# Another order of wave 0's half-block products and of the sums around them, in a linear-attention and MLP kernel

## The chip, the cores and the metric

The kernel runs on one core of one Trainium2 chip. A core has TensorE (PE; its weight loads are shown apart as PEld), VectorE (DVE), ScalarE (ACT), GpSimd (POOL) and SyncE (SP). Each takes its instructions strictly in the order in which the program lists them, and waits on semaphores for the others. The metric is the device time of one execution in microseconds (us). Three runs of the kernel before took 193.93 to 194.47 us, with a median of 194.27.

## The reference

Attention with a decay over blocks, then an MLP. What is computed, cut to the core:

```python
# q, k, v: 4 batches, 8 heads, 768 tokens, 64 columns; blocks of 64 tokens; lam: one decay per head
intra = einsum('bhic,bhjc->bhij', qb, kb) * Dmask      # Dmask[i, j] = lam ** (i - j) for i >= j
intra = einsum('bhij,bhjd->bhid', intra, vb)
inter = einsum('bhid,bhde->bhie', qb * lam_pow, kv_state)
out[:, :, sl] = intra + inter
kv_state = lam_block * kv_state + einsum('bhsd,bhse->bhde', kb_dec, vb)

x = out.transpose(0, 2, 1, 3).reshape(B * S, H * D)    # 3072 tokens, 512 columns
h = x @ w_in                                           # 512 x 2048
g = h * (1.0 / (1.0 + exp(-1.702 * h)))
result = g @ w_out                                     # 2048 x 512
```

## The kernel before, in words

The 3072 tokens are worked off in six waves of 512. For each wave the attention makes xT (x transposed), the first MLP product with the activation makes g (g_sb: 16 chunks of 128 hidden columns by 512 tokens, bf16), and the second product with w_out makes the output. Waves 0 and 1 hold two batches each with 256 tokens of each; the halves are called c = 0 and c = 1. While the second product of one wave runs, the attention of the next is worked in between its pieces. The order is written out by hand: `steps` reads strings of short names and calls one function for each, and the whole is under a manual schedule, so the order of the program is the order of each engine's queue.

**The second product.** g is seen as a 2 by 2 matrix of blocks (token half i, hidden half kh: a11, a12, a21, a22; hidden chunks with even number are the first half) and w_out as 2 by 2 blocks (hidden half, column half: b11 to b22). Instead of eight block products there are seven, by a scheme of Strassen's kind. It needs four sums of g (`g_sums`, L439, tile g_s: s1 = a21 + a22, s2 = s1 - a11, s3 = a11 - a21, s4 = a12 - s2) and four of w_out (`weight_sums`, L426, tile w_out_t: t1 = b12 - b11, t2 = b22 - t1, t3 = b22 - b12, t4 = b21 - t2), all on DVE. The products are

- 1: a11 b11, 2: a12 b21, 3: s4 b22, 4: a22 t4, 5: s1 t1, 6: s2 t2, 7: s3 t3.

`product` (L459) issues product n for token tiles t (0, 1) and hidden pairs m (0 to 7): one matmul of 128x128 by 128x256 for each, so 16 for a whole product. They add up in three PSUM banks: X takes 1, then 6, 5 and 3 on top; V takes 7, and then 4 from zero; Q takes 2. When the last matmul of a product is issued, `after_product` empties the bank: products 1, 6 and 7 are copied by ACT to an f32 tile (L472, tile part); product 2 is added to 1, 5 to 7, and 4 to 6 by DVE (L483, tile o_sb); 3 is copied by ACT (L481). The add of product 2 is put off until the step `o`; that of 4 waits until 6 is there. Each output block is stored by two DMAs issued on SP (L489). A product that goes on in the same bank waits until the bank has been read.

**Steps and names.** `P60` is product 6 for token tile 0, `P61` for tile 1. `p6...` takes both tiles and a part of the pairs: `a` is pairs 0 to 3, `b` 4 and 5, `l` 0 to 5, `h` 6 and 7. `gl3` makes s3 for pairs 0 to 3, `gh12` makes s1 and s2 for pairs 4 to 7. `W2` makes the sums of chunk 2 of w_out. w_out comes in four chunks of 512 KB by DMAs on POOL's queue (L185); chunk j serves pairs 2j and 2j + 1, so pairs 6 and 7 need the last chunk, number 3.

**Wave 1's attention** in between. `do_cast` (L202) multiplies q or k by its decay and casts it to bf16 (ks, qs), on DVE for c = 0 and on POOL for c = 1. `turn_pe` transposes the result by eight PE matmuls (L238) and a copy of ACT (kT, qT). `cast_v` casts v (on POOL for c = 0, on ACT for c = 1). `start` runs the first state products (`d_one`, L279) with ACT's copies of them, the scores (L259) with their masks on DVE (L267, tile sm), and the first part of the output (`d_even`, L298). `end` runs the rest of the output (`d_out`, L316), more state products, and the copies to xT. `load(2, "kq")` issues four loads of wave 2 on SP. `mlp1_half` (L414) is a part of the first MLP product of wave 1, and needs a PSUM bank of the three that X, V and Q use.

The steps 5 to 13 are worked between the pieces of wave 0's first MLP product, `mlp1(0, fc)`; the loop over `halves` is wave 1's first MLP product, which follows.

Of the kernel before, what the change touches and what calls it, by code (L numbers as in the profile page):

```python
# [25 lines left out]
def kernel(  # L26
# [391 lines left out]
    half_sum, blocks, part, c11, c12 = {}, {}, {}, {}, {}  # L418
    TS = [const.tile([P, FFC // 2, d_model // 2], bf16, name=f"w_out_t{n}") for n in range(1, 5)]

    def weight_sums(j):
        b = w_out_sb[j].rearrange("p (m two) (c d) -> p two c m d", two=2, c=2)
        t1, t2, t3, t4 = (t[:, j * CW // 2 : (j + 1) * CW // 2] for t in TS)
        for o, x, y in ((t1, b[:, 0, 1], b[:, 0, 0]), (t2, b[:, 1, 1], t1),
                        (t3, b[:, 1, 1], b[:, 0, 1]), (t4, b[:, 1, 0], t2)):
            nc.vector.tensor_tensor(o, x, y, op=SUB)  # L426

    def token_half(w, i, kh):
# [134 lines left out]
    def one_step(w, s):  # L563
        if s[0] == "+":
            w, s = w + 1, s[1:]
        x, a = w + 1, s[1:]
        if s[0] == "f":
            mlp1(w, int(a))
        elif s[0] in "abcd":
            k = "abcd".index(s[0])  # L570
            in_product(w, GR[w][k], int(s[1]), TAGS[w][k], dve_copy if s[2:] == "v" else act_copy)
        elif s[0] in "ABCD":
            in_gelu(w, GR[w]["ABCD".index(s[0])], int(a))
        elif s[0] == "P":
            product(w, int(s[1]), (int(s[2]),))
        elif s[0] == "p":
            product(w, int(s[1]), (0, 1), {"a": range(4), "b": range(4, 6), "l": range(6), "h": range(6, 8)}[s[2]])
        elif s[0] == "W":
            weight_sums(int(a))
        elif s[0] == "I":  # L580
            in_sums(int(a))
        elif s[0] in "kq":
            do_cast(x, int(a), s[0], nc.vector)
        elif s[0] in "KQ":
            do_cast(x, int(a), s[0].lower(), nc.gpsimd)
        elif s[0] == "t":
            turn_dma(x, int(s[2]), s[1])
        elif s[0] == "v":
            cast_v(x, int(s[1]), ((act_copy, dve_copy)[s[2:] == "v"],))
        elif s[0] == "S":  # L590
            n_scores(x, int(a))
        elif s[0] == "M":
            n_masks(x, int(a))
        elif s[0] == "m":
            n_masks(x, int(a), True)
        elif s[0] == "R":
            n_rest(x)
        elif s[0] == "o":
            c11.pop(w)()
        elif s[0] == "X":  # L600
            x_sums(x)
        elif s[0] == "G":
            gate_pool(x_sum[w][3][0:1, 0, 0:1])
        elif s[0] == "g":
            m0, m1 = {"l": (0, 4), "h": (4, 8)}[s[1]]
            g_sums(w, m0, m1, tuple(int(c) - 1 for c in s[2:]))
        elif s[0] == "L":
            load(w + (1 if a == "w" else 2), "kq" if a == "k" else "v")
        else:
            raise ValueError(s)  # L610
# [26 lines left out]
    with tc.manual_schedule():  # L637
        for x, i in ((k_pow, i_k), (q_pow, i_q)):
            nc.scalar.activation(x, ln_lam.unsqueeze(1).to_broadcast([P, 2, H]), EXP, scale=i)
        mk_pow(inv_pow, -1.0 * P)  # L640
        for j, rows in enumerate((A, Z)):
            nc.scalar.activation(blk_pow[rows].rearrange("p (r i) -> p r i", i=2),
                                 ln_lam[rows].rearrange("p (r j i) -> p r j i", i=2, j=2)[:, :, j, :], EXP, scale=1.0 * P)
        nc.scalar.activation(warm, q_pow[:, 0, 0:1], GELU)
        fill(3)
        for nm, copies in (("k", (dve_copy, act_copy)), ("q", (act_copy, dve_copy))):
            for g in range(2):
                do_cast(0, 0, nm, nc.vector, g)
            for g in range(2):
                turn_pe(0, 0, nm, copies[g], g)  # L650
                fill(2 - g if nm == "k" else 1 - g)
        gate_pool(loaded[0, 0, "q"][0:1, H // 2, 0:1])
        load_w_in(0)
        load_one(0, 1, "v", v)
        cast_v(0, 0, (act_copy, act_copy))
        d_scores(0, 0, 0)
        d_scores(0, 0, 1)
        fill(3)
        do_cast(0, 1, "k", nc.gpsimd, 0)
        load_w_in(1)  # L660
        do_cast(0, 1, "k", nc.gpsimd, 1)
        for j in range(2, len(IN_CH)):
            load_w_in(j)
        for j in range(NCH):
            load_w_out(j)
        d_one(0, 0, "mm")
        d_keep(0, 0)
        turn_pe(0, 1, "k", act_copy, 0)
        oa, oz = d_out(0, 0, ("mm", "mm"))
        nc.scalar.copy(seen, oz[:, 3, P - 1 : P])  # L670
        d_state(0, 0, states[0, 0], Z)
        do_cast(0, 1, "q", nc.vector, 0)
        do_cast(0, 1, "q", nc.vector, 1)
        d_x(0, 0, 0, oa, act_copy)
        turn_pe(0, 1, "q", act_copy, 0)
        d_inter(0, 0, oz, 0, False)
        turn_pe(0, 1, "k", dve_copy, 1)
        turn_pe(0, 1, "q", dve_copy, 1)
        d_x(0, 0, 1, oz, act_copy)
        fill(1, "a")  # L680
        d_scores(0, 1, 0, True)
        cast_v(0, 1, (act_copy, dve_copy))
        nc.gpsimd.affine_select(mask, mask, pattern=[[0, 1], [1, P]], channel_multiplier=-1, base=0,
                                compare_op=mybir.AluOpType.is_ge, fill=0.0)
        gate_sync(w_out_sb[1][0:1, 0, 0:2])
        load(1)
        d_scores(0, 1, 1, True)
        mlp1_half(0, 0, 0)
        d_one(0, 1)
        d_keep(0, 1)  # L690
        act_copy(kv_sb[0][:, 0], states[0, 0])

        def start(w, c):
            if c == 0:
                d_one(w, c)
                d_keep(w, c)
            for pp in range(2):
                d_scores(w, c, pp)
            d_even(w, c, ("mm", "a")[c])

        def end(w, c):
            oa, oz = d_out(w, c)
            t = acc("ps_kv", shape=[P, NP, D]) if w else states[w, c]
            if w == 0:
                nc.scalar.copy(seen, oz[:, 3, P - 1 : P])
            d_state(w, c, t, Z)
            if w == 0:
                d_inter(w, c, oz, 0, False)
            if w and c == 0:
                d_one(w, 1)  # L710
            d_x(w, c, 0, oa, act_copy)
            d_x(w, c, 1, oz, act_copy if w and c else dve_copy)
            if w:
                nc.vector.tensor_tensor(kv_sb[0][:, 2 * w + c], kept[w, c], t, op=ADD)
            else:
                nc.scalar.copy(kv_sb[0][:, 2 * w + c], t)
            if w and c == 0:
                d_keep(w, 1)

        def steps(w, names):  # L720
            for s in names.split():
                one_step(w, s)

        end(0, 1)
        for c, fc in ((0, 2), (1, 0), (1, 2)):
            mlp1_half(0, c, fc)
        for fc in range(4, FFC):
            mlp1(0, fc)
            steps(0, {5: "I1", 7: "I3", 9: "I0 gl3 gl1", 11: "W0 gl2", 13: "W1 gl4"}.get(fc, ""))
        steps(0, "p1a gh3 p2a W2 p1b p2b p7l W3 p1h p2h p7h")  # L730
        do_cast(1, 0, "k", nc.vector)
        steps(0, "p4l")
        do_cast(1, 0, "q", nc.vector)
        turn_pe(1, 0, "k", act_copy)
        steps(0, "p4h gh1 gh2 o")
        load(2, "kq")
        cast_v(1, 0)
        do_cast(1, 1, "k", nc.gpsimd)
        turn_pe(1, 0, "q", act_copy)
        steps(0, "P60")  # L740
        start(1, 0)
        steps(0, "P61 gh4")
        cast_v(1, 1, (act_copy, act_copy))
        do_cast(1, 1, "q", nc.gpsimd)
        turn_pe(1, 1, "k", act_copy)
        steps(0, "P50 P51")
        end(1, 0)
        turn_pe(1, 1, "q", act_copy)
        steps(0, "P30 P31")
        halves = [(c, fc) for c in range(HF) for fc in HALVES]  # L750
        for i, (c, fc) in enumerate(halves):
            if i == 1:
                start(1, 1)
            if i == 3:
                end(1, 1)
            if i == 4:
                x_sums(1)
            mlp1_half(1, c, fc)
            if i in (1, 2, 3, 4):
                nm = "kq"[(i - 1) % 2]  # L760
                do_cast(2, (i - 1) // 2, nm, nc.gpsimd)
                turn_dma(2, (i - 1) // 2, nm)
            if i == 6:
                load(2, "v")
        steps(1, STEPS[1])
        for w in range(ND, NW):
            steps(w, STEPS[w])
# [30 lines left out]
```

## Time and profile before

| | |
|---|---|
| time, median of 3 runs | 194.27 us |
| time of the profiled execution | 195.65 us |
| span of the profiled execution | 193.9 us |
| TensorE clock granted | 1.0 of full speed |
| PE busy | 185.0 us (95% of the span) |
| PEld busy | 151.6 us (78%) |
| DVE busy | 154.1 us (79%) |
| ACT busy | 129.9 us (67%) |
| POOL busy | 54.1 us (28%) |
| HBM read and written | 27.26 MB and 6.29 MB |

The span runs from the first to the last instruction; the time of an execution also holds what lies around it. In the profile's timelines a row has the start and the duration in us, the engine, the line of the kernel, the operation, the tile written and the tiles read, the sizes and the number of instructions taken together. Square brackets give the idle time just before, and what ended it. The end of a matmul is modelled, so the durations of neighbouring PE rows overlap.

The part of the program that the change touches lies between 26 and 53 us of the span.

### The profile page before, as it was taken

To read this page: it belongs to the slowest core of one execution; us is meant where nothing else is said; L and a number is where in the kernel's file an instruction comes from. 1 tells how busy PE (TensorE), PEld (TensorE's weight loads), DVE (VectorE), ACT (ScalarE), POOL (GpSimd) and SP (SyncE) were. 2 spreads that over 40 slices of the span, in tenths; PEclk is the share of its full clock that TensorE was granted. 3 is DMA by queue.
4 is the path that set the end of the run, shared out by engine and by line. 5 is a ranking of instruction groups with operands and counts; after the bars stand their busy time and mean duration, and the time that the engine had idled before them with its cause. 6 is when DMAs were issued, how large, how long until landed. Compare 5 with 4: busy or idle time off the path is not lost.

```text
span 193.9 us, 5541 instructions
## 1 busy us (share of the span) xinstructions
PE 185.0 (95%) x2295; PEld 151.6 (78%) x2297; DVE 154.1 (79%) x292; ACT 129.9 (67%) x242; POOL 54.1 (28%) x76
## 2 busy tenths in 40 slices
PE   7889999699999999999999999999999999999993
PEld 2556646577888887888888888888888888888882
DVE  1897599589377899988899979799979797889850
ACT  4867664246677885559796389896388885587711
POOL 4498000068476000088000096000294000000000
PEclk9999999999999999999999999999999999999999
DMA  5999999998997899657798935999455903300113
GB/s 148 306 275 196 201 194 213 290 299 215 224 248 168 193 249 236 163 137 137 178 237 189 270 110 134 208 246 231 163 150 125 211 7 109 111 3 0 47 43 130
DMA packets 89599, 33.91 MB, mean 175 GB/s; under 512 B 67430, under 2 KB 89446, under 8 KB 89574
## 3 DMA queue, kind: packets, MB, share of 16 engines
q1 hardware_dynamic: 84676, 28.84, 59.4%
q0 software_dynamic: 4896, 4.72, 14.4%
q8 instruction: 18, 0.29, 0.6%
q14 instruction: 7, 0.06, 0.1%
q10 hardware_dynamic: 2, 0.00, 0.0%
HBM read 27.26 MB, written 6.29 MB: 173 GB/s over the span
## 4 chain that ended last, share of the span: by engine, by line
PE 69%; DMA 12%; DVE 9%; POOL 5%; ACT 1%; issue 1%; SPq 1%; ACTq 0%
PE ps_X L459 19%; PE ps_hX L542 16%; DMA w_out<-in_moe_w_out_dram 10%; PE ps_hV L542 8%; PE ps_V L459 7%; PE ps_hQ L542 4%; PE ps_Q L459 4%; PE ps_h L414 4%; DVE g_s L439 3%; DMA qf<-in_q_dram 3%; POOL w_in L181 2%; PE ps_s L335 2%; PE ps_o L390 2%; POOL ks L202 1%; DVE sm L348 1%; POOL w_out L185 1%
## 5 line engine op out<-in xcount | busy, mean ns | idle before, releaser
L459 PEld LDWEIGHTS <-g_s 128*128 128x128 bf16 x384 | 36.8, 98 | 6.7 <-issue 1.2
L561 ACT ACTIVATE g_sb<-h_sb 128x512 bf16<-128x512 f32 x54 | 32.6, 631 | 1.2 <-DVE h_sb L550 1.2
L459 PEld LDWEIGHTS <-g_sb 128*128 128x128 bf16 x288 | 27.5, 98 | 5.9 <-issue 1.8
L542 PEld LDWEIGHTS <-w_in_t 128*128 128x128 bf16 x288 | 28.1, 98 | 3.3
L221 ACT COPY part<-ps_hX 128x512 f32<-128x512 f32 x32 | 18.3, 586 | 11.5 <-PE ps_hX L542 11.5
L459 PE MATMUL ps_X<-w_out_t,g_s 128*128 128x256 bf16 x192 | 23.5, 273 | 0.5 <-ACT part L472 0.2
L542 PEld LDWEIGHTS <-w_in 128*128 128x128 bf16 x216 | 21.1, 98 | 2.4
L542 PE MATMUL ps_hX<-x_s,w_in_t 128*128 128x256 bf16 x144 | 21.6, 272 | 0.0
L439 DVE TENSOR_TENSOR g_s<-g_sb 128x1024 bf16<-128x1024 bf16 x24 | 16.3, 688 | 5.8 <-ACT g_sb L561 5.6
L632 POOL CAST behind_q<-x_s 1x1 f32<-1x1 bf16 x3 | 0.5, 174 | 61.7 <-DVE x_s L527 61.7
L209 POOL TENSOR_TENSOR qs<-qf,q_pow 128x512 bf16<-128x512 f32 x16 | 16.6, 1063 | 2.7 <-DMA qf<-in_q_dram 2.7
L209 POOL TENSOR_TENSOR ks<-kf,k_pow 128x512 bf16<-128x512 f32 x16 | 16.6, 1063 | 1.9 <-DMA kf<-in_k_dram 1.9
L472 ACT COPY part<-ps_X 128x512 f32<-128x512 f32 (+1 forms) x14 | 7.3, 522 | 13.9 <-PE ps_X L459 13.9
L218 DVE COPY part<-ps_hV 128x512 f32<-128x512 f32 x18 | 12.4, 688 | 4.3 <-PE ps_hV L542 4.3
L550 DVE TENSOR_TENSOR h_sb<-part,ps_hX 128x512 f32<-128x512 f32 x18 | 12.3, 681 | 2.7 <-PE ps_hX L542 2.7
L459 PE MATMUL ps_X<-w_out,g_sb 128*128 128x256 bf16 x96 | 12.6, 273 | 0.8 <-DMA w_out<-in_moe_w_out_dram 0.8
L550 DVE TENSOR_TENSOR h_sb<-part,ps_hV 128x512 f32<-128x512 f32 x18 | 12.3, 684 | 1.0 <-PE ps_hV L542 1.0
L459 PE MATMUL ps_Q<-w_out,g_sb 128*128 128x256 bf16 x96 | 12.5, 273 | 0.0
L459 PE MATMUL ps_V<-w_out_t,g_sb 128*128 128x256 bf16 x96 | 11.8, 273 | 0.7 <-ACT part L472 0.7
L550 DVE TENSOR_TENSOR h_sb<-part,ps_hQ 128x512 f32<-128x512 f32 x18 | 12.2, 679 | 0.0
L267 DVE TENSOR_TENSOR sm<-ps_s,mask_d 128x512 bf16<-128x512 f32 x14 | 8.8, 684 | 3.8 <-PE ps_s L259 3.6
L459 PE MATMUL ps_V<-w_out_t,g_s 128*128 128x256 bf16 x96 | 11.6, 273 | 0.2 <-DVE w_out_t L426 0.2
(111 smaller groups left out, 360.5 us busy)
## 6 DMA issues: line engine op xcount, KB each, us to landing
kf<-in_k_dram SPq DMA_DIRECT2D x10, 512.0 KB, 6.6
qf<-in_q_dram SPq DMA_DIRECT2D x10, 512.0 KB, 6.6
vf<-in_v_dram SPq DMA_DIRECT2D x10, 512.0 KB, 6.0
out_dram<-o_sb SPq DMA_DIRECT2D x24, 128.0 KB, 2.4
out_dram<-o_sb SPq DMA_DIRECT2D x12, 256.0 KB, 2.7
w_out<-in_moe_w_out_dram POOLq DMA_DIRECT2D x4, 512.0 KB, 14.6
kf<-in_k_dram SPq DMA_DIRECT2D x4, 256.0 KB, 3.1
qf<-in_q_dram SPq DMA_DIRECT2D x4, 256.0 KB, 5.0
```

The costliest lines, as they stand in the source:

```text
L181: nc.gpsimd.dma_start(out=w_in_sb[j], in_=moe_w_in.rearrange("(kc ki) f -> ki kc f", ki=P)[:, :, c0 : c0 + IN_CH[j] * P])
L209: eng.tensor_tensor(x.rearrange("p b (r i j d) -> p j (b r) i d", i=2, j=2, d=D)[:, j], f.rearrange("p h (a d) -> p (h a) d", a=2).rearran ...
L218: nc.vector.tensor_copy(out, in_)
L221: nc.scalar.copy(out, in_)
L267: nc.vector.tensor_tensor(sm.rearrange("p i a s -> p i (a s)"), flat, mask_d.rearrange("p o a b s -> p o (a b s)").to_broadcast([P, 2, 2 * ...
L414: nc.tensor.matmul(h[:, u, :], w_in_sb[j][:, kc, i * P : (i + 1) * P], xT[w][:, kc, cols], start=(kc == 0), stop=(kc == KC - 1))
L439: nc.vector.tensor_tensor(o, x, y, op=f)
L459: nc.tensor.matmul(bank[:, t], x[:, m, t * P : (t + 1) * P], y, start=(n in (1, 2, 7) and t == ts[0] * last and m == 0), stop=(m == FFC // ...
L472: nc.scalar.copy(part[w, n, t.start][:, t], bank[:, t])
L542: nc.tensor.matmul(bank[:, u], z[:, kc], y[:, kc], start=(n in (1, 2, 7) and u + kc == 0), stop=(kc == 1), skip_group_check=True)
L550: nc.vector.tensor_tensor(h, h_part[w, g, {2: 1, 5: 7, 4: 6}[n]], bank, op=ADD)
L561: nc.scalar.activation(g_of[w][:, a : b + 1 : b - a, 256 * i : 256 * i + 256], bank, GELU)
```

## The change

- Wave 0's second product runs its products in the order 1, 2, 7, 6, 4, 5, 3 and no longer 1, 2, 7, 4, 6, 5, 3. Product 6 is now in two pieces by pairs, product 4 in three, and its last piece comes after the second turn.
- Products 5 and 3 are split differently around wave 1's work: tile 0 of product 5 comes ahead of `start(1, 0)`, tile 1 after it; tile 0 of product 3 stands ahead of the second turn of q, and tile 1 after the first piece of wave 1's first MLP product.
- `weight_sums` takes an order. Chunks 0 and 1 keep theirs; chunk 2 runs t3, t1, t2, t4; chunk 3 runs t3, t1, t2, and t4 only after wave 1's casts of k and q.
- s1 and s2 for pairs 4 to 7 are made ahead of chunk 3's sums; s4 for these pairs is made after chunk 3's t4.
- The cast of v's half c = 1 and POOL's cast of q now stand directly after `start(1, 0)`.

```diff
-    def weight_sums(j):
+    def weight_sums(j, which=(0, 1, 2, 3)):
         b = w_out_sb[j].rearrange("p (m two) (c d) -> p two c m d", two=2, c=2)
         t1, t2, t3, t4 = (t[:, j * CW // 2 : (j + 1) * CW // 2] for t in TS)
-        for o, x, y in ((t1, b[:, 0, 1], b[:, 0, 0]), (t2, b[:, 1, 1], t1),
-                        (t3, b[:, 1, 1], b[:, 0, 1]), (t4, b[:, 1, 0], t2)):
+        ops = ((t1, b[:, 0, 1], b[:, 0, 0]), (t2, b[:, 1, 1], t1),
+               (t3, b[:, 1, 1], b[:, 0, 1]), (t4, b[:, 1, 0], t2))
+        for i in which:
+            o, x, y = ops[i]
             nc.vector.tensor_tensor(o, x, y, op=SUB)
...
-            weight_sums(int(a))
+            weight_sums(int(a[0]), tuple(int(i) - 1 for i in a[1:]))
...
-            steps(0, {5: "I1", 7: "I3", 9: "I0 gl3 gl1", 11: "W0 gl2", 13: "W1 gl4"}.get(fc, ""))
-        steps(0, "p1a gh3 p2a W2 p1b p2b p7l W3 p1h p2h p7h")
+            steps(0, {5: "I1", 7: "I3", 9: "I0 gl3 gl1", 11: "W01234 gl2", 13: "W11234 gl4"}.get(fc, ""))
+        steps(0, "p1a gh3 p2a W23124 p1b p2b gh12 p7l W3312 p1h p2h p7h")
         do_cast(1, 0, "k", nc.vector)
-        steps(0, "p4l")
+        steps(0, "p6l p6h p4a")
         do_cast(1, 0, "q", nc.vector)
         turn_pe(1, 0, "k", act_copy)
-        steps(0, "p4h gh1 gh2 o")
+        steps(0, "p4b W34 gh4 o")
         load(2, "kq")
         cast_v(1, 0)
         do_cast(1, 1, "k", nc.gpsimd)
         turn_pe(1, 0, "q", act_copy)
-        steps(0, "P60")
+        steps(0, "p4h P50")
         start(1, 0)
-        steps(0, "P61 gh4")
         cast_v(1, 1, (act_copy, act_copy))
         do_cast(1, 1, "q", nc.gpsimd)
+        steps(0, "P51")
         turn_pe(1, 1, "k", act_copy)
-        steps(0, "P50 P51")
         end(1, 0)
+        steps(0, "P30")
         turn_pe(1, 1, "q", act_copy)
-        steps(0, "P30 P31")
         halves = [(c, fc) for c in range(HF) for fc in HALVES]
         for i, (c, fc) in enumerate(halves):
             if i == 1:
+                steps(0, "P31")
                 start(1, 1)
```

## The prediction

> **What bounds the kernel now.** I read the chain of waits first. TensorE (PE) holds most of it, and in waves 2 to 5 it is nearly all PE, so whatever PE loses earlier is lost for good. Up to 60 us the chain leaves PE in one place only, where wave 0's products wait for the last chunk of w_out:
>
> ```profile
> 17.62 18.74 DMA w_out<-in_moe_w_out_dram
> 36.39 0.44 DVE w_out_t L426
> ```
>
> From 36.39 to 42.30 the chain then runs on VectorE (DVE): sums of w_out, casts of k and q, sums of g. Next I read PE's timeline there (start, duration, line, output and inputs, count, idle before it):
>
> ```profile
> 34.13 1.47 PE L459 MATMUL ps_V<-w_out_t,g_s 128*128 128x256 bf16 x12
> 36.40 0.60 PE L459 MATMUL ps_X<-w_out,g_sb 128*128 128x256 bf16 x4 [0.80 <-DMA w_out<-in_moe_w_out_dram]
> ...
> 37.66 0.60 PE L459 MATMUL ps_V<-w_out_t,g_s 128*128 128x256 bf16 x4 [0.22 <-DVE w_out_t L426]
> 38.93 1.47 PE L459 MATMUL ps_V<-w_out_t,g_sb 128*128 128x256 bf16 x12 [0.67 <-ACT part L472]
> ...
> 41.56 1.34 PE L459 MATMUL ps_X<-w_out_t,g_s 128*128 128x256 bf16 x8
> 42.84 0.37 PE L279 MATMUL ps_kv<-v_sb,ks 64*64 64x64 bf16 x12
> ...
> 43.98 1.05 PE L459 MATMUL ps_X<-w_out_t,g_s 128*128 128x256 bf16 x8
> ...
> 45.70 1.91 PE L459 MATMUL ps_X<-w_out_t,g_s 128*128 128x256 bf16 x16 [0.23 <-ACT part L472]
> 47.53 0.64 PE L316 MATMUL ps_o<-sm,v_sb 64*64 64x128 bf16 x32
> ...
> 48.62 0.62 PE L238 MATMUL ps_t<-ident,qs 128*128 128x128 bf16 x8
> 49.08 1.91 PE L459 MATMUL ps_X<-w_out,g_s 128*128 128x256 bf16 x16
> 50.83 1.04 PE L414 MATMUL ps_h<-xT,w_in 128*128 128x256 bf16 x8
> 51.80 0.64 PE L259 MATMUL ps_s<-qT,kT 64*64 64x128 bf16 x32
> ...
> 52.48 1.92 PE L414 MATMUL ps_h<-xT,w_in 128*128 128x256 bf16 x16
> ```
>
> Ends on PE are modelled, so I measure from start to start. Sixteen product matmuls take 50.83 - 49.08 = 1.75, or 0.109 each (0.44 for four, 0.875 for eight); a turn takes 49.08 - 48.62 = 0.46. What the distance holds beyond this is a gap:
> - before 36.40: 2.27 less 12 matmuls = 0.96, for w_out;
> - 36.40 to 37.66: eight matmuls, 0.385 over (product 7 waits for t3, third of the sums);
> - 37.66 to 38.93: four, 0.83 over (product 4 overwrites product 7's bank V and waits for ACT's copy of it);
> - 41.56 to 42.84: eight, 0.405 over (half of product 6 waits for s2);
> - 43.98 to 45.70: eight and a turn, 0.385 over (product 5 waits for ACT's copy of product 6);
> - 45.70 to 47.53, 0.08, and 50.83 to 51.80, 0.095.
>
> After 36.40 that makes 2.18 us. It bounds what reordering can gain in this stretch; the 0.96 lies before it.
>
> **The change part by part.** The engines that feed these products:
>
> ```profile
> 36.39 0.43 DVE L426 TENSOR_TENSOR w_out_t<-w_out 128x512 bf16<-128x512 bf16 x1 [2.29 <-DMA w_out<-in_moe_w_out_dram]
> ...
> 37.86 1.43 DVE L202 TENSOR_TENSOR ks<-kf,kd_pow 128x256 bf16<-128x256 f32 x4
> 39.20 1.43 DVE L202 TENSOR_TENSOR qs<-qf,qd_pow 128x256 bf16<-128x256 f32 x4
> 40.54 0.69 DVE L439 TENSOR_TENSOR g_s<-g_sb 128x1024 bf16<-128x1024 bf16 x1
> 41.26 0.98 DVE L439 TENSOR_TENSOR g_s<-g_s,g_sb 128x1024 bf16<-128x1024 bf16 x1
> 42.17 0.68 DVE L483 TENSOR_TENSOR o_sb<-part,ps_Q 128x512 f32<-128x512 f32 x1
> 43.55 2.49 DVE L267 TENSOR_TENSOR sm<-ps_s,mask_d 128x512 bf16<-128x512 f32 x4 [0.71 <-PE ps_s L259]
> ...
> 46.55 0.72 DVE L439 TENSOR_TENSOR g_s<-g_sb,g_s 128x1024 bf16<-128x1024 bf16 x1
> ```
>
> ```profile
> 37.04 0.58 ACT L472 COPY part<-ps_X 128x512 f32<-128x512 f32 x1 [4.73 <-PE ps_X L459]
> ...
> 45.54 1.14 ACT L221 CAST v_sb<-vf 128x512 bf16<-128x512 f32 x2
> 46.58 1.01 ACT L221 COPY kT<-ps_t 128x1024 bf16<-128x1024 bf16 x1
> ...
> 49.70 1.02 ACT L221 COPY qT<-ps_t 128x1024 bf16<-128x1024 bf16 x1
> 51.03 0.58 ACT L481 COPY o_sb<-ps_X 128x512 f32<-128x512 f32 x1 [0.31 <-PE ps_X L459]
> ```
>
> ```profile
> 40.70 2.02 POOL L215 CAST v_sb<-vf 128x512 bf16<-128x512 f32 x2 [21.97 <-DMA vf<-in_v_dram]
> 42.68 2.32 POOL L202 TENSOR_TENSOR ks<-kf,kd_pow 128x256 bf16<-128x256 f32 x4
> 44.97 2.77 POOL L202 TENSOR_TENSOR qs<-qf,qd_pow 128x256 bf16<-128x256 f32 x4
> ```
>
> No instruction is added or removed: matmuls, sums, copies and DMAs are the same, in another order. Wave 0's first products still meet w_out at 36.40, so the 0.96 stays. From there I walk PE's new order.
>
> *gh1 and gh2 before W3.* They cost 0.69 each and run from about 33.7 to 35.1, inside DVE's idle 2.29. They would cost 1.4 at most if w_out came that much earlier.
>
> *t3 first.* It is ready at 36.39 + 0.43 = 36.82, and p7h starts at 37.28, when PE is free. The 0.385 goes.
>
> *Product 6 after product 7, instead of 4.* It needs s2 (35.1), t2 of the last chunk (third sum; about 37.6, needed at 39.0) and ACT's copy of product 1 (37.62). PE is there at 37.71, a cover of 0.09. The 0.83 goes: product 7 is copied under product 6.
>
> *Casts of k and q.* One sum fewer stands before them, but q's load hardly allows an earlier cast (SyncE's issue, then the time to landing in the DMA view of that moment):
>
> ```profile
> 31.21 0.51 SPq L84 DMA_DIRECT2D qf<-in_q_dram  x1
> qf<-in_q_dram SPq DMA_DIRECT2D x1, 512.0 KB, 7.9
> ```
>
> It lands at 39.11, against the cast's 39.20 before. q's cast thus ends at about 40.6; W34, gh4 and the o add follow it.
>
> *Product 4 in three pieces.* Product 6 ends at 39.46, p4a at 40.33, k's turn at 40.79, p4b at 41.23, q's turn (cast ready at 40.6) at 41.69, p4h at 42.13 (t4 ready at about 41), P50 at 43.00 (copy of product 6 long done). The 0.405 and the 0.385 go.
>
> *start(1,0).* It begins at 43.00 instead of 42.84. v's cast is done at 40.70 + 2.02 = 42.72 in both, so PE has done 16 more product matmuls in front of it. It takes 43.98 - 42.84 = 1.14, to 44.14. P51 ends at 45.02, k's second turn at 45.48 (POOL's cast is ready at 45.00).
>
> *A new wait.* d_out comes 16 matmuls sooner and meets the masks. They began 0.71 after the start of d_one, so now at 43.71, and take 2.49: 46.20. The last quarter of d_out could have begun at 45.84 and begins at 46.25: 0.41 lost. Queued behind it are the state products, P30 and the next turn; nothing else waits. end(1,0), 48.62 - 47.53 = 1.09, finishes at 46.98.
>
> *The rest.* P30 to 47.86 (product 5's add follows the masks, done at about 46.8), q's turn to 48.32 (POOL's cast ends at 44.97 + 2.77 = 47.74), mlp1_half to 49.19, P31 to 50.07, start(1,1) 0.68 to 50.75. The next mlp1_half takes the bank of X and waits for ACT's copy of product 3: 50.07 + 0.2 + 0.58 + 0.05 = 50.90. Another 0.15 lost.
>
> So the second mlp1_half of wave 1 starts at 50.90 instead of 52.48: **1.58 us gained**. The check: 2.18 less 0.41, 0.15 and rounding.
>
> *What moves on POOL and DVE.* In before, the last two sums of g met POOL's v cast (0.98 for one, instead of 0.69) and gh4 met POOL's q cast (2.77 for four, against 2.32 for the ks cast). Now W34 and gh4 meet the v cast instead, and the q cast is free. By these rows that is +0.3 on DVE, off the path, and -0.3 to -0.45 on POOL, off the path too. An upper bound: both sums ahead of POOL's cast in full, 0.43 + 0.69 = 1.1, minus the 0.28 by which v_sb is early, 0.8 on the path. I take 0, since the cast took 2.02 with 1.67 of such sums beside it.
>
> The Trainium skill, SBUF — State Buffer, section "Who interferes with whom", says that a VectorE instruction with two SBUF inputs and a GpSimd instruction that reads SBUF exclude each other for the whole of the one that came first. By that rule the sum would be near its 0.8 bound if POOL lost each time, a gain of 0.8. The trace shows lengthened instructions on both sides, which agrees in kind, but nothing near a whole instruction per meeting.
>
> *SP's queue.* The stores of product 2 come about 0.5 earlier, those of 4, 5 and 3 still stand after the four loads of wave 2 and before the transposes, so its order is the same. The first score matmuls of wave 2 need the last transpose:
>
> ```profile
> 62.56 1.26 SPq L245 DMA_TRANSPOSE qT<-qs  x1
> qT<-qs SPq DMA_TRANSPOSE x1, 2.8
> 67.74 0.62 PE L335 MATMUL ps_s<-qT,kT 64*128 64x128 bf16 x16
> ```
>
> It lands at 65.36; the scores would come at 67.74 - 1.58 = 66.16. The cover shrinks from 2.38 to 0.8 and holds.
>
> **The sum.** The span of the profiled execution is 193.9, its time 195.65, so 1.75 lie around the span. The changed kernel's would be 192.3 and 194.07. The median of the runs, 194.27, is 1.38 below the profiled time; I take the same 1.6 from it: **192.7 us**.
>
> **The rivals.**
> - *A gate on POOL or DVE takes back half.* The v cast is pushed by up to 0.8 (above), or the masks come later. For it: the covers of 0.09 and 0.28 are thin. Against: the same kinds of instruction met before. Gain 0.8, so 193.5.
> - *Wave 2's inputs are what counts.* Loads, casts and transposes of wave 2 keep their absolute times. If they slip by 1.6 beyond the 0.8 cover (2.4 in all), scores wait and the gain is gone: 194.2. Against: nothing in SP's order is late.
> - *ACT stuck behind a load: slower.* The cast of v's second half now follows the start's copies directly; before, product 6's copy stood between, at 45.06. ACT would wait for the load, with the turn's copy, xT, the state copies and qT behind it in order:
>
> ```profile
> 39.17 1.39 SPq L84 DMA_DIRECT2D vf<-in_v_dram  x1
> vf<-in_v_dram SPq DMA_DIRECT2D x1, 512.0 KB, 6.0
> ...
> vf<-in_v_dram SPq DMA_DIRECT2D x1, 512.0 KB, 8.8
> ```
>
>   It landed at 45.17. From there ACT has about 0.3 of slack up to product 3's copy, so the gain of 1.58 is used up when it lands 1.9 later, at 47.05; from then on the kernel is slower. With the 8.8 that the other half's load took (second line), it would land at 47.97: 194.27 + 0.92 = 195.2. Against: all that is queued before this load is unchanged.
> - *It does not do what it says.* The wait for w_out itself stays, as costed; were the three later gaps shadows of it rather than DVE and ACT waits, nothing would change. The rows name ACT and DVE as the releasers, so I fold this into the second rival.
>
> **How the numbers follow.** Forecast 0.74; half the gain 0.13; no change 0.07; slower 0.06. A measurement of this kernel tells from no change what is over 0.3%, 0.58 us, so faster begins below 193.69: 0.74 + 0.13 = 0.87 faster, 0.07 same, 0.06 slower. Low end: all 2.18 gained, 192.1. High end: a gain of 0.7, 193.6, which takes in the half-gain rival; what is left out is 0.13 and a little.
>
> **What would show it.** On PE: the wait for w_out unchanged at about 36.4, then no gap over 0.1 until d_out of wave 1; product 6 right behind 7; d_one at about 43.0; a gap of some 0.4 inside d_out released by the masks; the second mlp1_half at 50.9. On DVE: two sums of g within the wait for w_out. On POOL: the v cast ending at 42.7 and the q cast nearer 47.4. On ACT: the v cast starting on its DMA at about 45.2. Wrong would be d_one after 43.5, an ACT wait on vf beyond 46, or wave 2's first scores waiting for qT.

## The result, and the profile after

Twenty runs of the changed kernel took 192.43 to 194.78 us, with a median of **193.38**; twenty runs of the kernel before took 193.93 to 196.30, with a median of 194.86. The ratio is **0.9933**, with a 95% interval of 0.9909 to 0.9956. Of 194.86 that is 1.3 us less (0.9 to 1.8). Forecast were 1.58 us off the span and 192.7 us. The difference is right in kind and near in size. The absolute time is 0.7 higher than forecast, nearly all of it because the kernel before has a higher median over twenty runs (194.86) than over the three shown at first (194.27).

The profile's first part, span and engines:

```profile
span 192.1 us, 5543 instructions
...
PE 185.1 (96%) x2295; PEld 152.6 (79%) x2297; DVE 153.7 (80%) x292; ACT 129.7 (68%) x242; POOL 53.1 (28%) x76
```

PE's busy time is what it was (185.0 before); the span is 1.8 shorter. PE's timeline of the changed stretch, in the columns of before:

```profile
34.86 1.47 PE L461 MATMUL ps_V<-w_out_t,g_s 128*128 128x256 bf16 x12
36.17 0.60 PE L461 MATMUL ps_X<-w_out,g_sb 128*128 128x256 bf16 x4
...
37.04 0.60 PE L461 MATMUL ps_V<-w_out_t,g_s 128*128 128x256 bf16 x4
37.48 1.91 PE L461 MATMUL ps_X<-w_out_t,g_s 128*128 128x256 bf16 x16
39.23 1.04 PE L461 MATMUL ps_V<-w_out_t,g_sb 128*128 128x256 bf16 x8
...
41.87 1.04 PE L461 MATMUL ps_X<-w_out_t,g_s 128*128 128x256 bf16 x8
42.83 0.38 PE L279 MATMUL ps_kv<-v_sb,ks 64*64 64x64 bf16 x12
...
43.97 1.05 PE L461 MATMUL ps_X<-w_out_t,g_s 128*128 128x256 bf16 x8
44.85 0.61 PE L238 MATMUL ps_t<-ident,ks 128*128 128x128 bf16 x8
45.40 0.53 PE L316 MATMUL ps_o<-sm,v_sb 64*64 64x128 bf16 x24
46.08 0.31 PE L316 MATMUL ps_o<-sm,v_sb 64*64 64x128 bf16 x8 [0.16 <-DVE sm L267]
...
49.05 1.04 PE L461 MATMUL ps_X<-w_out,g_s 128*128 128x256 bf16 x8
50.02 0.64 PE L259 MATMUL ps_s<-qT,kT 64*64 64x128 bf16 x32
...
50.70 1.92 PE L414 MATMUL ps_h<-xT,w_in 128*128 128x256 bf16 x16
```

Product 6 starts 0.44 after product 7's last piece, without a gap; so does product 4 behind it. d_one comes at 42.83, where it also came before (42.84), with 16 more matmuls in front of it. The one new wait is in d_out: its first 24 matmuls end 0.36 after 45.40, the last eight start at 46.08, so 0.32 is lost to the masks. From the first product with w_out's last chunk (36.17, "p1h" below) to wave 1's second mlp1_half (50.70) it is **14.53 us; before it was 52.48 - 36.40 = 16.08**. This distance holds the changed stretch and leaves out PE's wait for w_out itself, so it is the measure in what follows; a wait for t3, which comes of a late w_out, still lies within it. It shrank by 1.55.

The wait of 0.96 for w_out is not in this execution: PE came to its first product of the wave at 32.24, 0.73 later than in before's, and w_out had landed. DVE, ACT and POOL beside it:

```profile
34.41 0.68 DVE L441 TENSOR_TENSOR g_s<-g_sb 128x1024 bf16<-128x1024 bf16 x1
35.12 0.69 DVE L441 TENSOR_TENSOR g_s<-g_s,g_sb 128x1024 bf16<-128x1024 bf16 x1
35.73 0.75 DVE L428 TENSOR_TENSOR w_out_t<-w_out 128x512 bf16<-128x512 bf16 x2
...
37.80 1.43 DVE L202 TENSOR_TENSOR ks<-kf,kd_pow 128x256 bf16<-128x256 f32 x4 [0.86 <-DMA kf<-in_k_dram]
...
40.95 1.10 DVE L441 TENSOR_TENSOR g_s<-g_sb,g_s 128x1024 bf16<-128x1024 bf16 x1
```

```profile
45.32 1.14 ACT L221 CAST v_sb<-vf 128x512 bf16<-128x512 f32 x2 [1.03 <-DMA vf<-in_v_dram]
```

```profile
40.83 1.69 POOL L215 CAST v_sb<-vf 128x512 bf16<-128x512 f32 x2 [22.93 <-DMA vf<-in_v_dram]
...
44.77 2.32 POOL L202 TENSOR_TENSOR qs<-qf,qd_pow 128x256 bf16<-128x256 f32 x4
```

The two sums of g now lie where DVE used to idle. The cast of k waits 0.86 for its load; my walk had put such a wait on q's load, not on k's, and q's cast starts at 39.26 as forecast (39.2). ACT stands idle for 1.03 until v's load has landed, and its cast of v starts at 45.32 (forecast 45.2).

### The profile page after: what moved, and what is told of

Its sections match the earlier page's. It is cut to its first block, busy times and chain, and to the rows that moved or that the text cites. A ratio compares the mean times of both kernels' runs of the same rounds, so it can differ in the third digit from the quotient of the medians.

```text
span 192.1 us, 5543 instructions
## 1 busy us (share of the span) xinstructions
PE 185.1 (96%) x2295; PEld 152.6 (79%) x2297; DVE 153.7 (80%) x292; ACT 129.7 (68%) x242; POOL 53.1 (28%) x76
## 4 chain that ended last, share of the span: by engine, by line
PE 80%; DVE 9%; DMA 4%; SPq 3%; issue 1%; ACT 1%; ACTq 0%
PE ps_X L461 20%; PE ps_hX L544 16%; PE ps_V L461 9%; PE ps_hV L544 8%; PE ps_h L402 5%; PE ps_h L414 5%; PE ps_Q L461 5%; PE ps_hQ L544 4%; DMA qf<-in_q_dram 4%; SPq L84 3%; DVE sm L267 2%; DVE g_s L441 2%; PE ps_s L335 2%; PE ps_o L390 2%; DVE sm L348 1%
## 5 line engine op out<-in xcount | busy, mean ns | idle before, releaser
L221 ACT CAST v_sb<-vf 128x1024 bf16<-128x1024 f32 (+1 forms) x13 | 11.3, 884 | 1.1 <-DMA vf<-in_v_dram 1.0
L461 PE MATMUL ps_X<-w_out,g_s 128*128 128x256 bf16 x96 | 11.6, 272 | 0.2 <-DVE o_sb L485 0.2
```

What stands on the lines that cost most here:

```text
L221: nc.scalar.copy(out, in_)
L461: nc.tensor.matmul(bank[:, t], x[:, m, t * P : (t + 1) * P], y, start=(n in (1, 2, 7) and t == ts[0] * last and m == 0), stop=(m == FFC // ...
```

## The experiments

Each experiment was timed against the kernel before on the same chip, with 6 to 12 executions, and profiled once. The table takes p1h, d_one and wave 1's second mlp1_half from PE's timeline in each profile, in us from the span's start; the distance is the last of these less the first, and the span is that of the profiled execution.

| kernel | ratio to before | 95% interval | p1h | d_one | 2nd mlp1_half | distance | span |
|---|---|---|---|---|---|---|---|
| before | 1 | | 36.40 | 42.84 | 52.48 | 16.08 | 193.9 |
| changed | 0.9933 | 0.9909 to 0.9956 | 36.17 | 42.83 | 50.70 | 14.53 | 192.1 |
| changed, again | 0.9935 | 0.9905 to 0.9964 | 37.12 | 43.79 | 51.66 | 14.54 | 193.0 |
| sums of g early alone | 0.998 | 0.9949 to 1.0011 | 35.15 | 41.26 | 51.05 | 15.90 | 192.4 |
| and 4 and 6 exchanged | 0.9936 | 0.9905 to 0.9966 | 36.81 | 41.95 | 51.38 | 14.57 | 192.8 |
| the same, again | 0.9959 | 0.9929 to 0.9990 | 36.37 | 42.15 | 52.01 | 15.64 | 193.4 |
| sums of w_out in old order | 0.9898 | 0.9868 to 0.9928 | 35.20 | 42.38 | 50.24 | 15.04 | 191.6 |
| product 5 behind start | 0.9892 | 0.9851 to 0.9933 | 35.21 | 41.00 | 49.81 | 14.60 | 191.2 |
| the same, again | 0.9919 | 0.9889 to 0.9950 | 35.97 | 41.77 | 50.50 | 14.53 | 191.9 |
| old tail | 0.9905 | 0.9868 to 0.9942 | 35.06 | 41.72 | 49.58 | 14.52 | 190.9 |
| product 5 behind, old tail | 0.9935 | 0.9904 to 0.9966 | 35.53 | 41.32 | 50.24 | 14.71 | 191.6 |
| v held back, changed | 0.9924 | 0.9894 to 0.9955 | 37.40 | 44.06 | 51.92 | 14.52 | 193.2 |
| v held back, before | 0.9983 | 0.9957 to 1.0010 | 35.23 | 41.77 | 51.41 | 16.18 | 192.7 |
| a mask in two steps | 0.9937 | 0.9901 to 0.9974 | 36.35 | 43.42 | 51.40 | 15.05 | 192.8 |

Three things stand out. p1h moves by 2.3 from one execution to another, and the spans of the changed kernel's twenty runs lie between 190.7 and 193.1, so a single span says little of an edit. The distance of the changed kernel is the same to 0.01 in two executions 0.95 apart in p1h (I had expected 14.4 to 14.7 of the second), though one execution is not always typical, as the two rows of the exchange show. And the span less the second mlp1_half is 141.3 to 141.4 in all fourteen profiles: nothing behind the stretch takes any of the gain back or adds to it, and a span differs from another only by p1h and the distance.

### The sums of g early, alone

```diff
-        steps(0, "p1a gh3 p2a W2 p1b p2b p7l W3 p1h p2h p7h")
+        steps(0, "p1a gh3 p2a W2 p1b p2b gh1 gh2 p7l W3 p1h p2h p7h")
...
-        steps(0, "p4h gh1 gh2 o")
+        steps(0, "p4h o")
```

> The kernel before, with only s1 and s2 of pairs 4 to 7 made ahead of the last chunk's sums of w_out. My theory: in front of wave 1's first state products (d_one) there is a fixed gate, POOL's cast of v, which ends at about 42.7 whatever PE does. Product 6 no longer waits 0.4 for s2, but PE then waits for v, so d_one still starts at 42.7 to 42.9, the second mlp1_half at 52.4 to 52.5, and the time is that of before (ratio 0.998 to 1.002). Rival, the sums are what gains: d_one at 42.4, 0.4 us faster.

```profile
35.15 0.60 PE L459 MATMUL ps_X<-w_out,g_sb 128*128 128x256 bf16 x4
...
37.61 1.47 PE L459 MATMUL ps_V<-w_out_t,g_sb 128*128 128x256 bf16 x12 [0.67 <-ACT part L472]
...
41.26 0.49 PE L279 MATMUL ps_kv<-v_sb,ks 64*64 64x64 bf16 x16
...
44.03 0.40 PE L238 MATMUL ps_t<-ident,ks 128*128 128x128 bf16 x4 [0.32 <-POOL ks L202]
```

The time is that of before within the interval, as my theory had it, but not for its reason: PE did not wait at d_one. It came at 41.26, 6.11 after p1h (6.44 before). v's cast ends at no fixed 42.7, but here at 41.29; PE, which was there at 41.17, met it almost exactly. The cast took 1.17 here and 2.02 before, since the early sums of g no longer fall into it (see the last section); with 2.02 it would have ended at 42.14. Of the 0.33 won in front of d_one, 0.15 is lost again behind it: k's second turn waits 0.48 for POOL, in place of product 5's wait for ACT. The wait of product 4 for ACT is untouched (0.67 by the row).

### Products 4 and 6 exchanged

Beside the edit above:

```diff
-        steps(0, "p4l")
+        steps(0, "p6l")
...
-        steps(0, "p4h o")
+        steps(0, "p6h o")
...
-        steps(0, "P60")
+        steps(0, "P40")
...
-        steps(0, "P61 gh4")
+        steps(0, "P41 gh4")
```

> The kernel before, with s1 and s2 early as in the first run and products 4 and 6 in each other's place; nothing else is moved. My theory: PE meets v's gate with the same 24 product matmuls done since product 7, stands idle for 0.7 to 1.1 us in front of d_one, which starts at 42.7 to 42.9 again; behind it only the 0.385 wait for the copy of product 6 and 0.08 go, so the second mlp1_half starts 9.2 after d_one (9.64 before, 7.87 after), and the gain is 0.5 us (ratio 0.996 to 0.999). Rival, the order of the products itself is what gains: 1.2 to 1.6 us, ratio 0.993.

```profile
36.81 0.60 PE L459 MATMUL ps_X<-w_out,g_sb 128*128 128x256 bf16 x4
...
37.73 0.60 PE L459 MATMUL ps_V<-w_out_t,g_s 128*128 128x256 bf16 x4
38.16 1.47 PE L459 MATMUL ps_X<-w_out_t,g_s 128*128 128x256 bf16 x12
...
41.95 0.44 PE L279 MATMUL ps_kv<-v_sb,ks 64*64 64x64 bf16 x16
...
44.60 1.91 PE L459 MATMUL ps_X<-w_out_t,g_s 128*128 128x256 bf16 x16
```

POOL's cast of v in the same run:

```profile
40.36 1.36 POOL L215 CAST v_sb<-vf 128x512 bf16<-128x512 f32 x2 [21.82 <-DMA vf<-in_v_dram]
```

My theory of a fixed gate fell here, and the rival was right in this execution: 14.57, with none of the finer pieces. Product 6 follows 7 at once, product 5 follows the turn at once, and d_one comes 5.14 after p1h because v was cast by 41.72, 4.91 after p1h, against 42.72 - 36.40 = 6.32 before. Of these 1.41, 0.75 is an earlier start of the cast (3.55 after p1h instead of 4.30) and 0.66 a shorter one (1.36 instead of 2.02).

> The kernel before, with s1 and s2 early and products 4 and 6 exchanged, once more. New theory: this exchange carries nearly all of the gain, since POOL's cast of v is done in time in most executions; the finer pieces of 4, 5 and 3 add something only where v lands late against w_out. Distance 14.5 to 15.0, ratio 0.991 to 0.996. Old theory, v's gate is fixed: distance 15.4 to 15.7, ratio 0.996 to 0.999.

```profile
36.37 0.60 PE L459 MATMUL ps_X<-w_out,g_sb 128*128 128x256 bf16 x4 [0.20 <-DMA w_out<-in_moe_w_out_dram]
36.80 0.60 PE L459 MATMUL ps_Q<-w_out,g_sb 128*128 128x256 bf16 x4
37.93 0.60 PE L459 MATMUL ps_V<-w_out_t,g_s 128*128 128x256 bf16 x4 [0.52 <-DVE w_out_t L426]
...
44.35 0.39 PE L238 MATMUL ps_t<-ident,ks 128*128 128x128 bf16 x4
44.99 0.40 PE L238 MATMUL ps_t<-ident,ks 128*128 128x128 bf16 x4 [0.25 <-POOL ks L202]
45.22 1.91 PE L459 MATMUL ps_X<-w_out_t,g_s 128*128 128x256 bf16 x16
```

In another execution the same kernel needed 15.64, a miss of my 14.5 to 15.0. That lies within the range of the old theory, but not by its mechanism: v was cast by 42.01 and d_one came at 42.15, as soon as PE was there. The 1.07 more is in two places: 37.93 - 36.80 = 1.13 where four matmuls take 0.44 (0.69 lost to t3, third of the sums, against 0.05 in the first execution), and 45.22 - 44.35 = 0.87 where a turn takes 0.46 (0.41 lost to POOL's cast of k, which had waited for its load). Both are covers that the whole change has and the exchange alone has not: t3 first, and sixteen matmuls more in front of the turn. The ratio, 0.9959, lies beside the changed kernel's 0.9935 on the same chip; the intervals overlap, so the time does not tell how much of the gain the exchange carries on average.

### The sums of w_out in the old order

The changed kernel with this edit:

```diff
-        steps(0, "p1a gh3 p2a W23124 p1b p2b gh12 p7l W3312 p1h p2h p7h")
+        steps(0, "p1a gh3 p2a W21234 p1b p2b gh12 p7l W31234 p1h p2h p7h")
...
-        steps(0, "p4b W34 gh4 o")
+        steps(0, "p4b gh4 o")
```

> The changed kernel, with the sums of w_out's chunks 2 and 3 in their old order t1, t2, t3, t4, and all four ahead of the casts (s1 and s2 still early). My theory: p7h waits 0.385 for t3 where w_out lands after PE is there (as in the profile of before), and nothing where PE is later than w_out (as in the profile of after); the cast of k waits for its load anyway. d_one at 42.8 to 43.2, 0 to 0.4 us lost, ratio 0.993 to 0.996. Rival, the order of these sums carries the gain: over 0.8 us lost.

```profile
35.64 0.60 PE L461 MATMUL ps_Q<-w_out,g_sb 128*128 128x256 bf16 x4
36.59 0.60 PE L461 MATMUL ps_V<-w_out_t,g_s 128*128 128x256 bf16 x4 [0.35 <-DVE w_out_t L428]
37.02 1.91 PE L461 MATMUL ps_X<-w_out_t,g_s 128*128 128x256 bf16 x16
```

From the first row to the last lie product 2's and product 7's four matmuls each, 0.875, but 37.02 - 35.64 is 1.38: 0.5 lost to t3, and a distance of 15.04 instead of 14.53. That is a little over my 0 to 0.4, and the rival's 0.8 is not reached. The ratio does not show this loss: it was to be 0.993 to 0.996 and was 0.9898, lower than the changed kernel's 0.9933. The changed kernel was not timed beside it on that chip, the two intervals overlap, and p1h alone moves executions by more than 0.5; so the cost in time of the old order stays open.

### Product 5 behind start, and the old tail

```diff
-        steps(0, "p4h P50")
+        steps(0, "p4h")
         start(1, 0)
...
-        steps(0, "P51")
+        steps(0, "P50 P51")
```

> The changed kernel, with both tiles of product 5 behind start(1, 0). My theory: 8 matmuls (0.875) leave the place in front of v's gate, PE waits there for 0.6 to 0.7, d_one starts at 42.7; but the masks are then done when d_out comes, so its wait of 0.32 goes too. The second mlp1_half starts at 50.9 to 51.1 (50.70 in the changed kernel): 0.2 to 0.4 us of the gain lost, ratio to before 0.994 to 0.997. Rival, moving product 5 forward is worth its whole length: 0.9 us lost.

```profile
41.00 0.22 PE L279 MATMUL ps_kv<-v_sb,ks 64*64 64x64 bf16 x2
41.47 0.41 PE L279 MATMUL ps_kv<-v_sb,ks 64*64 64x64 bf16 x14 [0.25 <-POOL v_sb L215]
...
44.86 0.64 PE L316 MATMUL ps_o<-sm,v_sb 64*64 64x128 bf16 x32
```

> The changed kernel with both tiles of product 5 behind start(1, 0), once more. New theory: the place of product 5 is worth nothing on average, because what PE waits less for the masks it may wait more for v: distance 14.4 to 15.0, ratio within 0.003 of the changed kernel's in the same job. Rival, from the first look's 0.989: this version is faster than the changed kernel by over 0.003.

The rows are from the first of the two runs. PE now waits some 0.4 at d_one for v (a row of two matmuls, then the rest 0.47 later), where I had expected 0.6 to 0.7, and d_out runs its 32 matmuls without a wait for the masks: the one wait for the other. The distances are 14.60 and 14.53, so the 0.2 to 0.4 that I had expected to be lost was not. In the second run its ratio was 0.9919 beside the changed kernel's 0.9935 on the same chip; the two intervals overlap over most of their length, so the lead of the first run is not borne out.

The old tail puts the turn of q directly behind `end(1, 0)`, product 3 whole behind it, and then the first mlp1_half.

> The changed kernel, with the end of wave 0 as it was: the second turn of q right behind end(1, 0), then both tiles of product 3, then wave 1's first mlp1_half. My theory: end(1, 0) is through at 46.9, POOL's cast of q at 47.1, so the turn waits 0.3 to 0.5 for POOL; the 0.1 that the second mlp1_half loses to the copy of product 3 goes. The second mlp1_half starts at 50.8 to 51.1, 0.1 to 0.4 us lost. Rival, ACT is the bound of this stretch: 0.8 us or more lost.

> The changed kernel with both tiles of product 5 behind start(1, 0) and the end of wave 0 as it was before (the turn of q, then product 3 whole, then mlp1_half). New theory: neither of these two edits of the change is worth anything; distance 14.3 to 14.8 and a ratio within 0.003 of the changed kernel's in the same job. Rival, the fine interleaving is worth 0.3 us or more: distance over 14.9.

The distances are 14.52 for the tail alone and 14.71 for both edits, with a ratio of 0.9935 for both beside the changed kernel's 0.9935 on the same chip. POOL's cast of q was done in time for the turn, so I had put the loss of the old tail 0.1 to 0.4 too high. Neither place is worth anything that these runs can tell.

### v held back

```diff
         do_cast(1, 0, "q", nc.vector)
+        gate_sync(cast[1, 0, "q"][0:1, 0, 0:2])
+        load_one(1, 1, "v", v)
```

(and the same load taken out of `load(1)`.)

> The changed kernel, with the load of v's second half of wave 1 issued on SP only once the cast of q on DVE is done (at about 41 instead of 39.3), so that it lands some 1.5 to 2 us later, at about 47. The theory that ACT's queue has little room: ACT's cast of v waits for it, d_one of c = 1 (the second half of the state products in end) waits for ACT, at 48.1 to 48.3 instead of 46.6, and the copies of kT, xT and qT queue behind. The second mlp1_half at 52.0 to 52.6, all or nearly all of the gain gone (ratio 0.998 to 1.002). Rival, ACT has room: under 0.5 us lost.

> The kernel before, with the same load held back in the same way. There d_one of c = 1 came at 48.4 only. The theory: a landing at about 47 costs it 0 to 0.5 us (ratio 1.000 to 1.003), so the changed kernel and this one come out within 0.5 us of each other. Rival, the late load costs both alike: 1.2 to 1.6 us, ratio 1.006 to 1.008.

This edit did not do what it was meant to. The load was issued at 41.42 in an execution in which p1h came at 37.40; ACT's cast began at 46.40, 9.0 after p1h, while in the changed kernel it was 45.32 - 36.17 = 9.15. Counted from p1h, the load was issued 0.9 later and landed as soon, 5.0 after its issue instead of 6.0; that it waited behind other transfers before would explain this, but is not shown. The distances (14.52, 16.18) are those without the edit, and the ratios were 0.9924 and 0.9983, both below the ranges of my theory. How much room ACT's queue has in front of a load that is really late was not measured.

### The last mask in two steps

```diff
-                d_scores(w, c, pp)
+                d_scores(w, c, pp, (w, c, pp) == (1, 0, 1))
```

> The changed kernel, with the last of the four masks of start(1, 0) made in two steps: ACT, which is idle there, copies the scores from PSUM to bf16, and DVE multiplies that in place by the mask. My theory: the last mask takes about 0.4 on DVE instead of 0.6 and is done at about 45.8, so the wait of 0.32 in d_out shrinks to 0.1; the second mlp1_half at 50.4 to 50.6. The gain is kept only if wave 2's first scores do not wait for the last transpose, which landed 0.3 ahead of them in the changed kernel: 0 to 0.3 us faster than that one. Rival, the multiply collides with POOL's cast of q and nothing is gained, or up to 0.3 lost.

```profile
36.55 0.69 DVE L441 TENSOR_TENSOR g_s<-g_s,g_sb 128x1024 bf16<-128x1024 bf16 x1
37.16 0.75 DVE L428 TENSOR_TENSOR w_out_t<-w_out 128x512 bf16<-128x512 bf16 x2
...
44.13 1.89 DVE L267 TENSOR_TENSOR sm<-ps_s,mask_d 128x512 bf16<-128x512 f32 x3 [0.72 <-PE ps_s L259]
45.94 0.80 DVE L267 TENSOR_TENSOR sm<-sm,mask_d 128x512 bf16<-128x512 bf16 x1
```

The rival was right: the multiply in SBUF took 0.80, more than the 0.62 of a mask from PSUM, while POOL's cast of q beside it took 2.50 instead of 2.32, and 0.12 of the distance is lost at the masks. What the multiply takes with POOL idle was not measured. But most of the 0.52 by which the distance is longer lies elsewhere, in the first two rows: here w_out's chunk 2 was late (PE waited 0.52 for it), the early sums of g ran until 37.2, and t3 of chunk 3 came behind them, 0.8 after p1h (36.35), so that product 7 waited 0.4. That is the price of moving these sums forward, in an execution like this one.

## Why the prediction was right

**The four gaps are real, and close for the reasons given.** 0.385 for t3, 0.83 for the copy of product 7, 0.405 for s2 and 0.385 for the copy of product 6 are gone in both profiles of the changed kernel. Taking the edits apart gives them back: t3 third costs 0.5 (old sums) to 0.69 (exchange, second run), and without the exchange the 0.67 wait for product 7's copy stays. Two of the gaps stand in for each other, though, which my list of terms does not say. The kernel before with v held back met an earlier w_out:

```profile
36.10 0.60 PE L459 MATMUL ps_V<-w_out_t,g_s 128*128 128x256 bf16 x4
...
40.02 0.60 PE L459 MATMUL ps_X<-w_out_t,g_s 128*128 128x256 bf16 x4
41.23 0.61 PE L459 MATMUL ps_X<-w_out_t,g_s 128*128 128x256 bf16 x4 [0.61 <-DVE g_s L439]
```

Product 7 did not wait for t3, but product 6 waited 0.77 for s2 (1.21 less four matmuls), about as much as 0.385 and 0.405 together, and the distance was 16.18. So t3 first would by itself have gained nothing in that execution. Product 4's three pieces and the earlier places of the two casts were not tried alone.

**The sizes held.** Counted from p1h, the second mlp1_half was forecast at 50.90 - 36.40 = 14.50 and came at 14.53 and 14.54; d_one at 6.60 and came at 6.66 and 6.67. d_out's loss was 0.41 and became 0.32. v's cast was to be done at about 42.7 and POOL's q cast nearer 47.4; they were at 42.52 and 47.09. The 0.15 for product 3's copy was not lost: the second mlp1_half starts 0.68 after the scores, as before. That the sum came within 0.03 all the same is in part luck. Where PE goes from a turn or from products to the attention's matmuls, some 0.09 goes by beyond the matmuls' own time (42.83 - 41.87 = 0.96 for eight, 45.40 - 44.85 = 0.55 for a turn, 50.02 - 49.05 = 0.97 for eight), as it did before (0.08 and 0.095). My walk left these three out, some 0.27 together, and they make up for the 0.09 and the 0.15. My signs of being wrong were put badly, in times of one execution: in the second profile of the changed kernel d_one came at 43.79 and ACT's cast of v at 46.14, past the 43.5 and the 46 that I had named, though counted from p1h they lie where they did in the first (6.67 and 9.02, against 6.66 and 9.15).

**The wait for w_out was not as steady as I put it.** I kept 0.96 on both sides. In the fourteen profiles PE's row of p1h names it with 0.80 (before), with 0.20 to 0.38 (six), or not at all (seven). I take it to belong to the execution and not to the order, so that it should cancel over many; the median gain of 1.48 beside the 1.55 of the distance agrees with that. But p1h moves single spans by more than the change does.

**The advance of product 5 was sized too high in my reasons, though not in the sum.** I read the gain as 16 more matmuls in front of a gate that v's cast sets, at 42.7 in both. The gate exists: it lies 6.0 to 6.7 after p1h in twelve of the profiles, and PE waits at it when product 5 stands behind `start`. But 4.9 and 5.6 in the two runs of the exchange show that it is not fixed: the cast starts 4.3 to 5.0 after p1h in thirteen profiles and 3.55 after it in one, and takes 1.17 to 2.08. What product 5 saves there d_out gives back at the masks. With product 5 behind `start` the distance is the same.

**The rivals.** In neither profile of the changed kernel is half the gain lost, or all of it, and ACT's wait for v's load ended at 45.32, far from the 47.05 at which the gain would have been used up. The one nearest to acting was wave 2's first scores (SyncE's issue, the DMA view of that moment, PE):

```profile
62.87 1.26 SPq L245 DMA_TRANSPOSE qT<-qs  x1
qT<-qs SPq DMA_TRANSPOSE x1, 2.8
65.96 0.62 PE L335 MATMUL ps_s<-qT,kT 64*128 64x128 bf16 x16
```

The last transpose landed at 65.67, so 0.29 was left of the cover of 2.38, less than the 0.8 I had left: SP issued the transposes 0.31 later, and the scores came 1.78 sooner, not 1.58. In the other profiles the cover lies between 0.2 (product 5 behind start) and 2.4, and in none do the scores wait. A further gain in front of this point may meet these transposes.

**The collision on DVE and POOL** was worth more than the zero I took. I read the cast of 2.02 as one that loses nothing by the sums beside it; where none falls into it, it takes 1.17. In before the collision lay on the path: s2 took 0.98 instead of 0.69, and PE waited for s2. In the changed kernel it is off the path, since v is cast 0.31 before d_one. In the run of the sums alone and in the exchange a cast of 2.02 would have ended 0.4 to 0.9 after d_one began, so there the shorter cast is part of what was won. See the last section.

## What to carry to other kernels

When two products go on in banks that an engine still has to empty, put between them one that goes on in another bank: here the exchange of two names, with its sums made in time, gave 1.51 in one run and 0.44 in another of the 1.55 that the whole change gave. Make the operand that is wanted first the first of its group, since its cover differs with each load's landing. Read a wait that ends on a DMA as one draw: judge an edit by a distance between two points inside the stretch, not by one span, and profile a second execution before calling a moment of the trace a fixed limit.

## What the runs showed of the hardware

POOL's cast of v is lengthened by DVE's sums of two SBUF operands that fall into it, and they by it:

```profile
40.12 1.17 POOL L215 CAST v_sb<-vf 128x512 bf16<-128x512 f32 x2 [21.60 <-DMA vf<-in_v_dram]
...
39.52 1.66 POOL L215 CAST v_sb<-vf 128x512 bf16<-128x512 f32 x2 [21.13 <-DMA vf<-in_v_dram]
...
40.94 2.08 POOL L215 CAST v_sb<-vf 128x512 bf16<-128x512 f32 x2 [22.45 <-DMA vf<-in_v_dram]
```

The first row is from the run with only the sums of g early, where no such sum falls into the cast: 1.17, as in the second run of the exchange. The second is from the run with the old order of w_out's sums, with one sum of g in it: 1.66. The third is the mask run. In the changed kernel the cast took 1.69, in before, with two sums of g, 2.02. The sum in turn took 1.10 instead of 0.69 in seven of the eight profiles with the change's order of these sums; in the eighth, the mask run, it took 0.69 and POOL's cast 2.08. Both ways the two lose 0.9 together: 0.41 and 0.52 in the changed kernel, nothing and 0.91 in the mask run. In before they lose 1.14 in two meetings (0.85 on the cast, 0.29 on a sum), 0.57 for each with a sum of 0.69, so I was wrong to find nothing near a whole instruction per meeting. The Trainium skill, SBUF — State Buffer, section "Who interferes with whom", says that such a pair of instructions excludes each other and the second waits the first one out. These rows agree with it in kind: what one side does not lose the other does, and the shares can change from run to run.
